# A list scheduler that orders by the array form of matmul groups and by a port that VectorE and GpSimd share

## The chip, the core and the metric

The kernel runs on one core of a Trainium2 chip. A core has a matrix engine (TensorE, PE in the views), a vector engine (VectorE, DVE), an activation engine (ScalarE, ACT), a general engine (GpSimd, POOL) and a queue engine for transfers (SyncE, SP). Each engine takes its instructions in the order in which they were written for it and waits by semaphores for what other engines make. The metric is the device time of one execution in microseconds, the median of several runs.

## The reference

What is computed, cut to what matters:

```python
# q, k, v, alpha: (4, 8, 768, 48), float32
for t in range(S):                                   # gated linear attention, per batch and head
    state = alpha[:, :, t, :, None] * state + einsum('bhd,bhe->bhde', k[:, :, t], v[:, :, t])
    y[:, :, t] = einsum('bhd,bhde->bhe', q[:, :, t], state)
x = y.transpose(0, 2, 1, 3).reshape(B, S, 384)
logits = x @ w_gate                                  # mixture: best 2 of 4 experts, softmax over the two
for e in range(4):                                   # each expert is one causal attention head of width 64
    q, k, v = x @ wq[e], x @ wk[e], x @ wv[e]
    a = softmax(causal(q @ k.T / 8))
    out += gate_weight[e] * (a @ v @ wo[e])
```

## The kernel before

**The linear attention** runs in 24 chunks of 128 time steps (4 batches of 6), all 8 heads at once, four head pairs on the partitions. For chunk `n`, `prep_r` (line 386) and `prep_c` (407) scan the gates backwards and forwards on VectorE (lines 393 and 416) and scale keys and queries with the results (420, 424). `gla_a` (439) makes the products of queries and keys on TensorE (445) into two PSUM buffers; one is masked by VectorE (454, tile `ms`), the other is copied by ScalarE (457) and masked by GpSimd (461). `gla_t` (468) transposes the keys (472), `gla_u` (480) makes the chunk's state (490; VectorE 504 or 508, GpSimd 511), and `gla_y` (515) the chunk's output (535), which is split into a high part `xh` (ScalarE, 544) and a low part `xl` (VectorE, 548) for the projections.

**The mixture** runs in 8 units of 384 rows (two for each batch; an odd unit also sees the keys of the even unit before it). `proj` (557) makes queries and keys of a pair of experts (567, nine matmuls of 384 columns), `vproj` (579) values and gate logits (585), `gate` (593) the gate weights on VectorE. For each pair of experts and each block of 128 rows `score` (625) makes the scores (642), VectorE adds the mask and takes the row's extreme (652), ScalarE takes the exponential and its sum (661), `norm` (665) makes a factor on VectorE (673, 674) and GpSimd scales the rows by it (680). `transp` (687) transposes them on TensorE (698), ScalarE copies them to `at` (712), `av` (720) multiplies them with the values (735), and `outp` (750) projects the sum (760); the result goes out by a transfer (767) from one of two buffers `ot`.

**Three forms of the matmul array.** By their `tile_position` the groups use the array in parts: 445 and 642 (in the code `pa`, `sc`) split its rows in two; 490 (`pu`) and 735 (`yv`) split its columns in two, 535 (`py`) in four; 472, 698, 567, 585 and 760 (`pt`, `tr`, `pj`, `pv`, `po`) use it whole. A float32 matmul that is no transposition counts twice in the views of the profile.

**What sets the order.** `build` (301) writes all steps down as operations of a `Plan` (59), each with its engine, an estimated occupancy and latency, and the buffers that it reads and writes. `mix` (842) interleaves the streams of operations (the rest of one unit, the projections of the next, the chunks of the one after it) by weights (`MIX_...`, lines 37 to 45); in `back` (782) the constant `AHEAD` (35) says after how many further blocks of scores a block is transposed. `schedule` (105) then plays a clock for each engine: among the operations whose inputs are there it takes, on each engine, those that could start within `LOOK` of the earliest, and of these the one that was written first. Buffers come from pools: seven PSUM buffers `g`, and SBUF pools such as `al`, `qk`, `a`, `ot`, which are given out strictly in the written order. The order in which operations are chosen is the order in which each engine gets its instructions (`emit`, 206); before the planned time 45 it fills TensorE's planned gaps with small matmuls that only keep it busy (`warm`, 941). The line that chooses:

```python
lo = min(x[0] for x in c)
t, i = min((x for x in c if x[0] <= lo + LOOK), key=lambda x: x[1])
```

## Time and profile before

| | us |
|---|---|
| median of 3 runs | 363.74 (363.12 to 364.96) |
| the profiled execution | 362.71 |
| its span, first to last instruction | 361.0 |

| engine | busy, us | share of the span | instructions |
|---|---|---|---|
| TensorE | 337.9 | 94% | 3686 |
| VectorE | 244.3 | 68% | 692 |
| ScalarE | 216.3 | 60% | 543 |
| GpSimd | 124.7 | 35% | 190 |

The profiled execution lies 1.71 us over its span and 1.03 us under the median. A share is an average over the whole span; the views by stretch, of waits and of the chain of work that ended last tell which engine the others wait for at a place. Ends of matmuls are modelled, so how long a group of matmuls holds the engine is read from the start of its first to the start of the next group's first.

### The profile page before, as it was taken

How to read it: one execution, taken by the hardware profiler on the slowest of the kernel's cores; microseconds unless marked ns; L12 is line 12 of the kernel's file. 1: busy time of each engine (PE TensorE's matmuls, PEld its weight loads, DVE VectorE, ACT ScalarE, POOL GpSimd, SP SyncE). 2: the span in 40 equal slices, each digit the busy share in tenths (PEclk: the TensorE clock that was granted, in tenths of full speed). 3: DMA queues.
4: the chain of work that ended last, by engine and by line, in shares of the span. 5: the costliest groups of instructions: out<-in, count | busy, mean ns of one | idle time of the engine just before them, and what ended most of it. 6: DMA issues, size and time to landing. Idle time of an engine off the chain costs nothing.

```text
span 361.0 us, 9454 instructions
## 1 busy us (share of the span) xinstructions
PE 337.9 (94%) x3686; PEld 264.9 (73%) x3686; DVE 244.3 (68%) x692; ACT 216.3 (60%) x543; POOL 124.7 (35%) x190
## 2 busy tenths in 40 slices
PE   8898898999899799999979999999999999999992
PEld 6678776887666587887857787877877797876682
DVE  6889999999999954665788843556266621448620
ACT  1554478754687445775548656675368564757960
POOL 4243249312485401441337321441056300423520
PEclk9999999999999989999999999999999999999997
DMA  7998333435223020423132320312100000100101
GB/s 193 272 268 213 108 108 107 134 107 149 81 78 107 27 82 27 147 78 100 35 96 83 107 58 25 118 42 70 67 3 2 2 2 3 65 1 2 65 24 54
DMA packets 13797, 29.85 MB, mean 83 GB/s; under 512 B 1616, under 2 KB 4912, under 8 KB 13744
## 3 DMA queue, kind: packets, MB, share of 16 engines
q1 hardware_dynamic: 13744, 29.16, 28.3%
q8 instruction: 31, 0.51, 0.6%
q14 instruction: 22, 0.18, 0.2%
HBM read 24.44 MB, written 4.72 MB: 81 GB/s over the span
## 4 chain that ended last, share of the span: by engine, by line
PE 54%; DVE 30%; issue 5%; ACT 4%; DMA 3%; POOL 1%; ACTq 0%; DVEq 0%; POOLq 0%
PE g L735 9%; PE g L698 9%; PE g L567 8%; PE g L642 8%; DVE al L416 6%; PE g L535 6%; PE g L760 5%; DVE al L393 5%; PE g L585 4%; DVE a L652 4%; PE g L445 3%; DVE qk L424 2%; DMA al<-in_al_dram 2%; DVE qk L420 2%; DVE ms L454 2%
## 5 line engine op out<-in xcount | busy, mean ns | idle before, releaser
L680 POOL TENSOR_SCALAR a<-a,cf,gw 128x128 f32<-128x128 f32 (+5 forms) x96 | 78.4, 827 | 130.3 <-DVE cf L674 85.8
L661 ACT ACTIVATE a<-a,mx 128x128 f32<-128x128 f32 (+5 forms) x96 | 63.2, 660 | 18.2 <-DVE mx L652 16.2
L652 DVE CUSTOM_DVE_ANT_0 a<-g,cm 128x384 f32<-128x384 f32 (+3 forms) x96 | 47.8, 530 | 35.0 <-PE g L642 30.7
L712 ACT ACTIVATE at<-g 128x512 f32<-128x512 f32 (+3 forms) x124 | 49.5, 456 | 7.8 <-PE g L698 7.7
L642 PE MATMUL g<-k,q 64*128 64x256 f32 (+3 forms) x256 | 49.7, 478 | 2.1 <-ACT ot L765 2.0
L698 PE MATMUL g<-ident,a 128*128 128x128 f32 x336 | 49.2, 283 | 1.8 <-POOL a L680 1.5
L698 PEld LDWEIGHTS g<-ident,a 128*128 128x128 f32 x336 | 38.1, 143 | 13.5 <-POOL a L680 5.1
L735 PE MATMUL g<-at,vg 128*64 128x384 f32 (+2 forms) x324 | 41.4, 393 | 1.4 <-ACT at L712 1.4
L535 PE MATMUL g<-ms,vt 128*32 128x128 f32 x768 | 36.0, 277 | 6.4 <-DVE ms L454 4.7
L436 ACT ACTIVATE al<-al 112x1033 f32<-112x1033 f32 x24 | 25.7, 1071 | 25.3 <-DVE qk L424 18.4
L393 DVE TENSOR_TENSOR_SCAN al<-al,d1r 112x516 f32<-112x516 f32 (+1 forms) x25 | 30.4, 1217 | 10.3 <-DMA al<-in_al_dram 10.3
L735 PEld LDWEIGHTS g<-at,vg 128*64 128x64 f32 x324 | 22.0, 136 | 20.3 <-issue 13.3
L567 PE MATMUL g<-xh,wqk_h 128*128 128x384 f32 x96 | 35.2, 367 | 0.5 <-DVE xl L548 0.5
L535 PEld LDWEIGHTS g<-ms,vt 128*32 128x32 f32 x768 | 23.4, 109 | 15.8 <-DVE ms L454 5.9
L567 PE MATMUL g<-xl,wqk_h 128*128 128x384 f32 x96 | 32.4, 338 | 0.5 <-DVE xl L548 0.5
L642 PEld LDWEIGHTS g<-k,q 64*128 64x128 f32 x256 | 22.5, 185 | 13.8 <-issue 4.6
L416 DVE TENSOR_TENSOR_SCAN al<-al,d1c 112x516 f32<-112x516 f32 (+1 forms) x25 | 32.1, 1283 | 0.8
L567 PE MATMUL g<-xh,wqk_l 128*128 128x384 f32 x96 | 32.4, 337 | 0.0
L511 POOL TENSOR_TENSOR S<-st,ev 48x192 f32<-48x192 f32 x32 | 21.2, 663 | 28.0 <-DVE st L508 26.8
L445 PE MATMUL g<-qk 48*128 48x128 f32 x384 | 28.1, 284 | 0.6 <-DVE qk L424 0.4
L535 PE MATMUL g<-qk,S 112*32 112x128 f32 x480 | 26.9, 275 | 0.0
L445 PEld LDWEIGHTS g<-qk 48*128 48x128 f32 x384 | 23.8, 187 | 4.0 <-issue 1.3
(91 smaller groups left out, 613.2 us busy)
## 6 DMA issues: line engine op xcount, KB each, us to landing
qk<-in_qk_dram SPq DMA_DIRECT2D x23, 448.0 KB, 4.0
vt<-in_v_dram SPq DMA_DIRECT2D x24, 256.0 KB, 4.1
al<-in_al_dram SPq DMA_DIRECT2D x23, 226.2 KB, 2.8
out_dram<-ot SPq DMA_DIRECT2D x24, 192.0 KB, 1.9
at<-in_wqk_dram SPq DMA_DIRECT2D x1, 768.0 KB, 11.4
qk<-in_qk_dram SPq DMA_DIRECT2D x2, 224.0 KB, 3.4
at<-in_wvg_dram SPq DMA_DIRECT2D x1, 390.0 KB, 10.7
at<-in_wo_dram SPq DMA_DIRECT2D x1, 384.0 KB, 11.5
```

Of the source, the lines that this page charges most:

```text
L393: V.tensor_tensor_scan(backwards(al[0:P, AW + c0 - 1:AW + c1 - 1]), backwards(al[0:P, c0:c1]), d1r[0:P, sl].rearrange("p a w -> p (a w)"), ...
L416: V.tensor_tensor_scan(c, c, T(("d1c", n))[0:P, sl].rearrange("p a w -> p (a w)"), 0.0, OP.mult, OP.max)
L445: PE.matmul(T(("pa", n, s))[:, C * p:C * p + C], t[r:r + D, p, C:2 * C], t[r:r + D, p, 0:C], start=True, stop=True, tile_position=(r, 0))
L535: PE.matmul(py[32 * j:32 * j + 32, k], l, r, start=(i == 0), stop=(i == len(parts) - 1), tile_position=(0, 32 * j))
L567: PE.matmul(pj[:, :W3], w[:, kt, cs], x[:, kt, :], start=(i == 0), stop=(i == 8))
L642: PE.matmul(T(sk[e])[:, :w], q[r, ts], k[r, c0:c1], start=True, stop=True, tile_position=(64 * e, 0))
L652: V.tensor_tensor_reduce(T(ak[e])[:, c0:c1], T(sk[e])[:, :w], cm[:, m0:m0 + w], -1.0, mx[:, 0:1] if x else BIG, OP.add, OP.min, accum_out= ...
L661: A.activation(a[:, 0:n], a[:, 0:n], AF.Exp, bias=T(mk)[:, e, len(pieces) - 1:len(pieces)], scale=-1.0, accum_out=T(("sm", u))[:, ix:ix + 1])
L680: G.tensor_scalar(a[:, 0:n], a[:, 0:n], T(ck_)[:, e:e + 1], T(("gw", u))[:, i, eg:eg + 1], op0=OP.mult, op1=OP.mult)
L698: PE.transpose(pt[:, 128 * (j - j0):128 * (j - j0) + 128], a[:, 128 * j:128 * j + 128], ident)
L712: A.activation(dst, src, AF.Copy)
L735: PE.matmul(py[64 * e:64 * e + 64, lo:n1], v[:, j % 3, 64 * eg:64 * eg + 64], at[e][:, at_off(j) + lo:at_off(j) + n1], start=(j == 0), sto ...
```

## The change

The scheduler's model is changed, and with it the order of the instructions; the operations, their sizes and their number stay the same, except for the small matmuls that fill planned gaps (88 before, 117 after).

- A TensorE operation carries the name of its form (`pe=`). `MODE` puts the forms in three classes, rows, columns and whole; between two classes the scheduler adds a time (`LEAVE` plus `ENTER`) to the start, and among the operations that could start within `LOOK` it takes one of the current class before one of another (`STICK`). The fixed 0.1 that each group's occupancy held before is gone.
- A VectorE operation with `port=True` and every GpSimd operation take turns on one modelled port (`port_at`).
- `use=` names the buffers of an operation's product, the one that a later operation copies out of PSUM: they are claimed with the operation itself, and other users of the buffer follow that one (`claims`).
- Successors on the same engine other than TensorE wait for the end of the latency (`SAME`); some occupancies are changed; the start of the plan (`ISSUE`) goes from 3.0 to 0.9.
- `AHEAD` goes from 3 to 2, and the weights of `mix` are other ones.

```diff
-AHEAD = 3
+AHEAD = 2
-MIX_BACK = (12, 20, 12, 20, 14, 20)
-MIX_FRONT = (16, 9, 11, 10, 12, 9)
+MIX_BACK = (10, 20, 8, 19, 13, 20)
+MIX_FRONT = (17, 7, 13, 10, 12, 9)
...
-MIX_GLA = 12
+MIX_GLA = 25
...
-ISSUE = 3.0
+ISSUE = 0.9
 SEM = 0.07
+SAME = 0.02
+STICK = 100
...
+MODE = {"pa": "row", "sc": "row", "pu": "col", "py": "col", "yv": "col"}
+ENTER = {"pa": 0.10, "sc": 0.104, "py": 0.024, "pu": 0.0, "yv": 0.05, "tr": 0.055, "pt": 0.055}
+LEAVE = {"pu": 0.064, "py": 0.11}
...
-    def op(self, eng, occ, lat, fn, r=(), w=(), dma=0):
+    def op(self, eng, occ, lat, fn, r=(), w=(), use=(), dma=0, port=False, pe=None):
...
+        keys += [k for k in use if k not in keys]
...
-            self.touch.setdefault(k, []).append(i)
+            t = self.touch.setdefault(k, [])
+            if t and k[0] in self.kinds:
+                claims.add(t[0])
+            t.append(i)
...
+        state = ["pj"]
+
+        def change(o):
+            a, b = state[0], o["pe"]
+            if MODE.get(a) == MODE.get(b):
+                return 0.0
+            return LEAVE.get(a, 0.096) + ENTER.get(b, 0.105)
...
             t = max(rt[i], at[o["eng"]])
+            if o["port"]:
+                t = max(t, port_at)
+            if o["pe"]:
+                t = max(rt[i], t + change(o))
...
-                    t, i = min((x for x in c if x[0] <= lo + LOOK), key=lambda x: x[1])
+                    c = [x for x in c if x[0] <= lo + LOOK]
+                    if e == "PE":
+                        t, i = min(c, key=lambda x: x[1] + STICK * (MODE.get(ops[x[1]]["pe"]) != MODE.get(state[0])))
+                    else:
+                        t, i = min(c, key=lambda x: x[1])
...
+            if o["port"]:
+                port_at = max(port_at, end - 0.03)
+            if o["pe"]:
+                state[0] = o["pe"]
...
-                op("PE", m * 0.109 + 0.1, m * 0.109 + 0.27, f, r=[(("a", u, pair, i, e), "s"), (("ident",), None)],
-                   w=whole(tk) + [(("at", u, pair, e), "slot")])
+                op("PE", m * 0.109, m * 0.109 + 0.17, f, pe="tr", r=[(("a", u, pair, i, e), "s"), (("ident",), None)],
+                   w=whole(tk), use=[("at", u, pair, e)])
```

**Two places in the order.** The first is TensorE at the last scores of unit 1 (`k_105` and `q_103` are the second pair's keys and queries, `a_136` the scaled rows that are transposed, 445 and 480, 535 and 571, 642 and 679 the same lines before and after). Before:

```order
L698 MATMUL g_67<-ident,a_136 128x128 x4
L698 MATMUL g_66<-ident,a_136 128x128
L642 MATMUL g_63<-k_105,q_103 128x256
L642 MATMUL g_64<-k_105,q_103 128x256
L642 MATMUL g_65<-k_105,q_103 128x512
L642 MATMUL g_69<-k_105,q_103 128x512
L535 MATMUL g_68<-ms_90,vt_80 32x128 x4
L535 MATMUL g_68<-qk_76,S_94 32x128 x4
L535 MATMUL g_68<-ms_90,vt_80 32x128 x4
L535 MATMUL g_68<-qk_76,S_94 32x128 x4
L535 MATMUL g_68<-ms_90,vt_80 32x128 x8
L535 MATMUL g_68<-qk_76,S_94 32x128 x4
```

and in the changed kernel:

```order
L480 MATMUL g_68<-qk_77 128x128
L480 MATMUL g_69<-qk_77 128x128
L679 MATMUL g_65<-k_105,q_103 128x512
L679 MATMUL g_67<-k_105,q_103 128x512
L679 MATMUL g_63<-k_105,q_103 128x256
L679 MATMUL g_64<-k_105,q_103 128x256
L679 MATMUL g_66<-k_106,q_100 128x128
L679 MATMUL g_69<-k_106,q_100 128x128
L571 MATMUL g_68<-ms_90,vt_80 32x128 x4
L571 MATMUL g_68<-qk_76,S_94 32x128 x4
L571 MATMUL g_68<-ms_90,vt_80 32x128 x4
L571 MATMUL g_68<-qk_76,S_94 32x128 x4
```

These scores now follow products of a chunk (480) and are followed by the next unit's first scores, all of the form with split rows; before they stood between transpositions and a chunk's output, one score block in its form by itself.

The second is VectorE ahead of the masked products of chunk 11 (`ms_91` in both). Before, with the forward scan of chunk 17 (`al_71`) ahead of it:

```order
L393 SCALAR_TENSOR_TENSOR al_71<-al_71,d1r 112x516
L397 RECIPROCAL d1c_87<-al_71 112x4
L416 SCALAR_TENSOR_TENSOR al_71<-al_71,d1c_87 112x516
L745 TENSOR_TENSOR yl_143<-g_67,yh_141 128x384
L454 TENSOR_TENSOR ms_91<-g_66,mask 128x512
```

and in the changed kernel, where `al_71` holds chunk 13 and `al_72` chunk 14 (428 and 451 are the scans, 544 the state, 781 the low part of a unit's output, 489 the masked products):

```order
L451 SCALAR_TENSOR_TENSOR al_71<-al_71,d1c_87 112x516
L428 SCALAR_TENSOR_TENSOR al_72<-al_72,d1r 112x516
L544 TENSOR_TENSOR st_93<-g_66,S_94 48x192
L781 TENSOR_TENSOR yl_143<-g_67,yh_141 128x384
L489 TENSOR_TENSOR ms_90<-g_64,mask 128x512
L544 TENSOR_TENSOR st_93<-g_66,S_94 48x192
L489 TENSOR_TENSOR ms_91<-g_68,mask 128x512
```

VectorE's preparation of chunks runs six chunks ahead of the masked products before, and three after.

## Rows read from the trace of the kernel before

**Rows 1.** The page's first part: busy time, share of the span and instructions of each engine.

```profile
PE 337.9 (94%) x3686; PEld 264.9 (73%) x3686; DVE 244.3 (68%) x692; ACT 216.3 (60%) x543; POOL 124.7 (35%) x190
```

**Rows 2.** Busy time of each engine in four stretches of the span: to the first projection, to the output of chunk 11, to the last matmul of the output, and the end. Columns: length, then busy time and number of instructions of PE, PEld, DVE, ACT and POOL, the granted clock as a share of full speed, DMA share and GB/s.

```profile
0.00:26.80 26.80, 23.18 (x341) 18.33 (x341) 21.07 (x36) 11.07 (x19) 9.26 (x27) 1.00 0.93 244
26.80:127.20 100.40, 91.03 (x1079) 71.79 (x1076) 97.72 (x231) 61.25 (x150) 44.68 (x58) 1.00 0.40 110
127.20:354.10 226.90, 223.49 (x2268) 174.72 (x2268) 125.39 (x426) 143.46 (x374) 70.72 (x106) 0.99 0.17 53
354.10:361.00 6.90, 0.21 (x3) 0.09 (x2) 0.15 (x1) 0.49 (x1) 0.00 (x0) 0.71 0.14 43
```

**Rows 3.** The chain of work that ended last, in order of time, where it passes from VectorE to TensorE: start, length, what.

```profile
124.42 1.55 DVE al L416
126.56 0.61 DVE ms L454
127.21 2.26 PE g L535 x56
129.48 4.09 PE g L698 x26
```

**Rows 4.** Timeline of TensorE about 325 us: start, modelled length, operation, sizes, count. A pair of scores of 512 columns is x4, one of 256 columns x4 too.

```profile
323.12 1.13 PE L642 MATMUL g<-k,q 64*128 64x512 f32 x4
324.18 0.55 PE L698 MATMUL g<-ident,a 128*128 128x128 f32 x3
...
327.38 2.42 PE L642 MATMUL g<-k,q 64*128 64x512 f32 x12
329.73 0.65 PE L698 MATMUL g<-ident,a 128*128 128x128 f32 x4
```

**Rows 5.** The chain of work again, from 196 to 219 us, where every piece is TensorE's: start, length, line and number of matmuls.

```profile
196.88 0.70 PE g L642 x4
197.58 1.28 PE g L585 x9
...
201.84 1.46 PE g L698 x12
203.30 1.09 PE g L585 x9
...
205.98 3.38 PE g L735 x24
209.36 1.77 PE g L567 x9
...
211.56 1.68 PE g L535 x56
213.24 1.13 PE g L698 x9
214.37 1.57 PE g L567 x9
215.95 1.86 PE g L698 x17
```

**Rows 6.** Timeline of TensorE at two places where the same group of 735 is followed by two others, of two and of four column parts.

```profile
159.77 1.52 PE L735 MATMUL g<-at,vg 128*64 128x384 f32 x12
161.11 0.53 PE L490 MATMUL g<-vt,kt 128*48 128x48 f32 x16
...
72.50 1.52 PE L735 MATMUL g<-at,vg 128*64 128x384 f32 x12
73.95 0.43 PE L535 MATMUL g<-ms,vt 128*32 128x128 f32 x8
```

**Rows 7.** Timeline of TensorE, two rows with the idle time before them and what ended it.

```profile
127.21 0.43 PE L535 MATMUL g<-ms,vt 128*32 128x128 f32 x8 [3.08 <-DVE ms L454]
...
184.03 1.55 PE L642 MATMUL g<-k,q 64*128 64x512 f32 x6 [1.97 <-ACT ot L765]
```

**Rows 8.** Stretches of 2 us behind the first of these waits, columns as in Rows 2.

```profile
128.00:130.00 2.00, 2.00 (x39) 1.61 (x32) 1.71 (x3) 0.47 (x1) 0.00 (x0) 0.57 0.03 8
...
132.00:134.00 2.00, 2.00 (x19) 2.00 (x18) 0.00 (x0) 2.00 (x7) 0.00 (x0) 1.00 0.57 180
```

**Rows 9.** VectorE's work for a chunk, groups by line and shape: operation, names, shapes, count, busy us, mean ns of one, idle us before and what ended it.

```profile
L416 DVE TENSOR_TENSOR_SCAN al<-al,d1c 112x516 f32<-112x516 f32 x23 | 30.5, 1328 | 0.8
L393 DVE TENSOR_TENSOR_SCAN al<-al,d1r 112x516 f32<-112x516 f32 x23 | 29.0, 1263 | 9.3 <-DMA al<-in_al_dram 9.3
L420 DVE TENSOR_TENSOR qk<-qk,al 112x512 f32<-112x512 f32 x23 | 17.2, 749 | 6.1 <-DMA qk<-in_qk_dram 6.0
L424 DVE TENSOR_TENSOR qk<-qk,al 112x512 f32<-112x512 f32 x23 | 16.3, 709 | 0.0
```

**Rows 10.** Groups by line and shape on the way from the scores to the transpositions, for rows of 768 columns, columns as in Rows 9.

```profile
L680 POOL TENSOR_SCALAR a<-a,cf,gw 128x768 f32<-128x768 f32 x16 | 16.5, 1043 | 19.7 <-DVE cf L674 9.9 <-ACT at L712 4.7 <-PE g L642 2.7
L661 ACT ACTIVATE a<-a,mx 128x768 f32<-128x768 f32 x16 | 14.8, 927 | 2.4 <-DVE mx L652 2.0
L652 DVE CUSTOM_DVE_ANT_0 a<-g,cm,mx 128x256 f32<-128x256 f32 x32 | 14.3, 476 | 0.0
L661 ACT ACTIVATION_READ_ACCUMULATOR a<-a,mx 128x1 f32 x96 | 18.0, 188 | 0.0
L673 DVE TENSOR_SCALAR cf<-sm 128x2 f32<-128x2 f32 x48 | 9.8, 204 | 13.9 <-ACT a L661 13.7
```

More of the change, by code (lines that the diff above doesn't have):

```diff
@@ L98, in op @@
         for k in keys:
-            self.touch.setdefault(k, []).append(i)
-        self.ops.append(dict(i=i, eng=eng, occ=occ, lat=lat, fn=fn, preds=preds, keys=keys, dma=dma))
+            t = self.touch.setdefault(k, [])
+            if t and k[0] in self.kinds:
+                claims.add(t[0])
+            t.append(i)
+        self.ops.append(dict(i=i, eng=eng, occ=occ, lat=lat, fn=fn, preds=preds, claims=claims - preds, keys=keys, dma=dma, pe=pe,
+                             port=port or eng == "G"))
         if eng == "PE":
@@ L123, in schedule @@
         for o in ops:
-            miss.append(len(o["preds"]))
-            for j in o["preds"]:
+            miss.append(len(o["preds"]) + len(o["claims"]))
+            for j in o["preds"] | o["claims"]:
                 succ[j].append(o["i"])
@@ L192, in schedule @@
             for j in succ[i]:
-                same = ops[j]["eng"] == e and not o["dma"]
-                rt[j] = max(rt[j], t + o["occ"] if same else end + SEM)
+                if i in ops[j]["claims"]:
+                    rt[j] = max(rt[j], t)
+                elif ops[j]["eng"] != e or o["dma"]:
+                    rt[j] = max(rt[j], end + SEM)
+                else:
+                    rt[j] = max(rt[j], t + o["occ"] if e == "PE" else end + SAME)
                 miss[j] -= 1
@@ L294, in pol @@
     def pol(n):
-        return 0.3 + n / 1150, 0.32 + n / 1150
+        return 0.31 + n / 1150, 0.33 + n / 1150
     def whole(*keys):
@@ L398, in prep_r @@
             occ = 0.08 + (c1 - c0) * 0.00206
-            op("V", occ, occ + 0.09, f, r=[(("al", n), ("c", p)) for p in ps_] + whole(("d1r",)),
+            op("V", occ, occ + 0.09, f, port=True, r=[(("al", n), ("c", p)) for p in ps_] + whole(("d1r",)),
                w=[(("al", n), ("s", p)) for p in ps_])
@@ L446, in f @@
                                   start=True, stop=True, tile_position=(r, 0))
-            op("PE", 1.1, 1.3, f, r=[(("qk", n), (x, p)) for x in "kq" for p in range(4)],
-               w=whole(("pa", n, 0), ("pa", n, 1)))
+            op("PE", 0.9, 1.17, f, pe="pa", r=[(("qk", n), (x, p)) for x in "kq" for p in range(4)],
+               w=whole(("pa", n, 0), ("pa", n, 1)), use=[("ms", n)])
             for s in (0, 1):
@@ L475, in g @@
                 A.activation(T(("kt", n)), T(("pt", n))[:, 0:4 * P].rearrange("p (a b) -> p a b", a=4), AF.Copy)
-            op("PE", 0.485, 0.65, f, r=[(("qk", n), ("k", p)) for p in range(4)] + whole(("ident",)),
-               w=whole(("pt", n)))
+            op("PE", 0.385, 0.55, f, pe="pt", r=[(("qk", n), ("k", p)) for p in range(4)] + whole(("ident",)),
+               w=whole(("pt", n)), use=[("kt", n)])
             op("A", *act(448), g, r=whole(("pt", n)), w=whole(("kt", n)))
@@ L540, in gla_y @@
                 r += whole(("S", n))
-            op("PE", occ, occ + 0.17, f, r=r, w=whole(("py", n)))
+            op("PE", occ, occ + 0.17, f, r=r, pe="py",
+               w=whole(("py", n)), use=[("xh", u), ("xl", u)])
             def fh(T):
@@ L568, in f @@
                         i += 1
-            op("PE", 1.67, 1.83, f, r=xs(u) + [(("wqk_h",), None), (("wqk_l",), which)],
-               w=whole(("pj", u, pair, which)))
+            op("PE", 1.57, 1.73, f, pe="pj", r=xs(u) + [(("wqk_h",), None), (("wqk_l",), which)],
+               w=whole(("pj", u, pair, which)), use=[("k", b, pair) if which else ("q", u, pair)])
             if which == 0:
@@ L643, in f @@
                                   tile_position=(64 * e, 0))
-                occ = 2 * (0.008 + w / 1200) + 0.1
-                wr = whole(*sk)
-                if x == 0:
-                    wr = wr + [(ak[0], "slot"), (ak[1], "slot"), (mk, "slot")]
-                op("PE", occ, occ + 0.17, f, r=whole(("q", u, pair)) + [(("k", b, pair), h) for h in range(hf + 1)], w=wr)
+                occ = 2 * (0.008 + w / 1200)
+                op("PE", occ, occ + 0.17, f, pe="sc", r=whole(("q", u, pair)) + [(("k", b, pair), h) for h in range(hf + 1)],
+                   w=whole(*sk), use=ak + [mk])
                 for e in (0, 1):
@@ L674, in f @@
                 V.reciprocal(cf, cf)
-            op("V", 0.24, 0.3, f, r=[(("sm", u), i0), (("sm", u), i0 + 3)], w=whole(ck_))
+            op("V", 0.29, 0.36, f, r=[(("sm", u), i0), (("sm", u), i0 + 3)], w=whole(ck_))
             for e in (0, 1):
@@ L737, in f @@
                                   start=(j == 0), stop=(j == nj - 1), tile_position=(0, 64 * e))
-            occ = 0.1 + sum(2 * (0.008 + (n1 - max(n0, 128 * (j - 3 * hf))) / 1200) for j in range(nj))
+            occ = sum(2 * (0.008 + (n1 - max(n0, 128 * (j - 3 * hf))) / 1200) for j in range(nj))
             r = whole(*[("vg", 2 * b + h) for h in range(hf + 1)])
@@ L741, in av @@
                   if j0 < 3 * hf + i + 1]
-            op("PE", occ, occ + 0.17, f, r=r, w=whole(yk))
+            op("PE", occ, occ + 0.17, f, r=r, pe="yv",
+               w=whole(yk), use=[("yh", u, pair), ("yl", u, pair)])
             op("A", *act(n1 - n0), lambda T: A.activation(T(("yh", u, pair))[:, ns], T(yk)[:, ns], AF.Copy),
@@ L762, in f @@
                         m += 1
-            op("PE", 1.14, 1.3, f, r=[((x, u, pair), i) for x in ("yh", "yl") for pair in (0, 1)]
-               + whole(("wo_h",), ("wo_l",)), w=whole(("po", u, i)))
+            op("PE", 1.05, 1.22, f, pe="po", r=[((x, u, pair), i) for x in ("yh", "yl") for pair in (0, 1)]
+               + whole(("wo_h",), ("wo_l",)), w=whole(("po", u, i)), use=[("ot", u, i)])
             op("A", *act(W3), lambda T: A.activation(T(("ot", u, i)), T(("po", u, i))[:, 0:DM], AF.Copy),
```

51 lines of the change are left out of this document (26 added, 25 removed).

## Prediction

> **What bounds the kernel now.** I read the page's busy shares first [rows 1]: TensorE is busy 94% of the span, VectorE 68%, so TensorE is the first suspect; but a share is a mean, so the stretches come next [rows 2]. To 127.2 us VectorE is the busier one: of the 100.4 us behind the first projection it works 97.7 and TensorE 91.0. Behind that TensorE works 223.5 of 226.9 us and VectorE 125.4. The chain of waits says the same: it runs through VectorE's scans until the masked products of chunk 11, and through TensorE from 127.21 on [rows 3]. There TensorE had stood idle for 3.08 us [rows 7], and in the 2 us from 128 its granted clock was 0.57, between the levels 1.2 and 2.4 GHz, and 1.00 again from 132 [rows 8]. So there are two stretches with different limits, VectorE's to 127.2 and TensorE's to 354.1, and 6.9 us of ending that no step here touches.
>
> A busy TensorE isn't one that computes all the time. A pair of scores of 512 columns alone takes 324.18 - 323.12 = 1.06 us from start to next start; a run of two such pairs and one of 256 columns takes 329.73 - 327.38 = 2.35 [rows 4]. With g for the pair and s for what a run costs however long it is, g + s = 1.06 and 2.5 g + s = 2.35: g = 0.86, s = 0.20. That s is the price of changing the array's form.
>
> **The change part by part.** No computation is removed, so everything hangs on the order.
>
> *Changes of form.* I counted in the two orders how often a TensorE group follows one of another form, with two and four column parts as two forms: 201 before, 96 after. The prices are from the chain, whose pieces run from the end of one group to the end of the next, so that the whole price lies in the group entered [rows 5]. Values' projections take 1.28 us behind scores and 1.09 behind transpositions; queries' and keys' projections 1.77 behind 735 and 1.57 behind transpositions: 0.19 to 0.20. Nine transpositions behind 535 take 1.13, and seventeen behind a projection 1.86, which is 0.109 each, so nine should take 0.98: 0.15. Scores, and likewise the products of a chunk, cost 0.20 [rows 4]. The column forms are priced by 735, which takes 73.95 - 72.50 = 1.45 us when the four-part 535 follows, and 161.11 - 159.77 = 1.34 when the two-part 490 follows [rows 6]: 0.11, and I take 0.12. By what is entered: rows split, 62 to 23, 39 x 0.20 = 7.8; projections, 32 to 11, 21 x 0.195 = 4.1; transpositions, 47 to 14, 33 x 0.15 = 5.0; columns split, 60 to 48, 12 x 0.12 = 1.4. Together 18.3 us of TensorE. With every change at the cheapest price (0.11) it would be 11.6, with every one at 0.20 21.0. Up to the output of chunk 11 the count falls from 71 to 35 (6.3 us at these prices), behind it from 130 to 61 (12.0 us).
>
> The scheduler's own classes hold two and four column parts for one form, and by them the counts are 193 and 78. Those rows show that a change between them costs the same 0.11. The Trainium skill's page "TensorEngine Tiling (Array Packing)", section Tiling Modes, says that changing the tiling mode, not just the tile, drains TensorE, and lists 128x64 and 128x32 as different configurations; the rows agree, and by the scheduler's classes the saving would be 115 changes, some 1.2 us more.
>
> *What stands ahead of chunk 11 on VectorE.* It was the later engine there. In the new order there stand ahead of `ms` of chunk 11 three reverse and four forward scans fewer (3 x 1.263 + 4 x 1.328 = 9.1 us), two pairs of products with keys and queries fewer (2 x 1.458 = 2.9) [rows 9], and four reductions of scores (0.476 for the shape in rows 10), four reciprocals, an `xl` and a pair of factors, some 3: 15 us in all. Up to 127.2 VectorE stood idle 26.8 - 21.1 + 100.4 - 97.7 = 8.4 us [rows 2]; with the same idle time it reaches that point at 127.2 - 15 = 112.2.
>
> *What stands ahead of chunk 11 on TensorE.* The same groups but for one projection, one score block and five transposition groups more, which comes to 3.3 us moved forward (1.57 for the projection [rows 5], some 1.7 for the rest at 0.109 a transposition and 0.86 for 512 columns of scores), and 36 changes of form fewer. TensorE idled 100.4 - 91.0 = 9.4 us there. Without any of it, it reaches chunk 11's output at 127.2 - 6.3 + 3.3 - 9.4 = 114.8; with all of it at 124.2. VectorE's 112.2 is no longer the later one, but two engines that are loaded alike, and wait for each other's buffers, lose some: I take a third of the 9.4 back, **118**. The ends are 114.8 and 124.2. The first 26.8 us hang on VectorE, busy for 21.1 of them [rows 2], whose order hardly moves there, and stay; the 29 more filling matmuls are written only where the plan has a gap, and I put them at nothing; where there is no gap they cost 0.107 us each, a quarter of the 0.43 that the four passes of a 256-column pair take [rows 4], 3.1 us at most.
>
> *Behind chunk 11.* 226.9 - 12.0 - 3.3 = 211.6. Of the idle 3.4 us there, 1.97 stood behind a transfer out of `ot` [rows 7]; the new claims let an output projection start only when its `ot` is free, so other groups go ahead. The clock's fall cost the 26 transpositions 4.09 - 26 x 0.109 = 1.25 us [rows 3], which goes with the wait that caused it. Against these 3.2 stands the shorter look-ahead (`AHEAD` 2): from a block's last scores to its transpositions TensorE's other work is, by order and durations, an estimate of 7.9 us in the middle and 4.1 at the least, before 11.7 and 3.1. For 768 columns the way between takes at least 0.48 (reduction) + 2 x (0.93 + 0.19 to read the sum out) + 0.40 (factor and its reciprocal, taken as equally long) + 1.04 (scaling) = 4.2 us [rows 10], and more when an engine is held up. I put some 4 us of new waits there. So 211.6 - 3.2 + 4.4 = 212.8, with the tight groups' waits between 0 and 12.
>
> **Sum.** 118 + 212.8 = 330.8 for the last matmul in place of 354.1: 23.3 us less. The profiled execution took 362.71 and would take 339.4; the median, 1.03 above it, **340.4**.
>
> **The rivals.**
>
> *VectorE stays the bound in the first stretch.* For it: it had only 2.7 idle us in 100, and scans are stretched when GpSimd works beside them (1.55 us in rows 3 against a mean of 1.33), which an order doesn't forbid. Then chunk 11 is reached at some 125, and waits of 4 us more follow behind it since units come late: 125 + 216.8 = 341.8 for the last matmul, 12.3 less: 351. Against it: 15 us of its work move behind that point by the order itself.
>
> *Still more is gained.* If the two engines mesh in the first stretch (114.8) and no wait comes behind it (211.6 - 3.2 = 208.4): 323.2, 30.9 less, 333. The rows speak against so smooth a run: TensorE had 9.4 us of waits there even with VectorE working throughout.
>
> *Slower: the softmax doesn't come back in time.* With look-ahead 2, and scores gathered in runs, a run's blocks reach VectorE, ScalarE and GpSimd together, and the last of them comes back latest; the transpositions at the head of TensorE's queue hold up everything behind them, the projections too. The 24 blocks of the odd units have the longest way (4.2 us and more, as above, against an estimate of 4 to 9 of cover). The gain of 23.3 is gone when each waits 0.97 us longer; at 1.5 us each it is 340.4 + 36 = 376, and idle times as long as the one at 127 would bring the clock's fall as well. Against it: where the way is longest the cover is mostly longer, and a wait once taken gives the next blocks time.
>
> *No change.* It would need the waits to grow by just what the changes of form give. That the kernel doesn't do what it says is excluded for the order, which shows 96 changes.
>
> **How the numbers follow.** The forecast's neighbourhood (335 to 346) 0.5; below 335 0.13; VectorE's bound or more waits (346 to 362) 0.25; no change 0.04; slower 0.08. A measurement of this kernel tells about 0.5% from no change, 1.8 us; faster by more than that has 0.88, within it 0.04, slower 0.08. The range leaves out the best end of the gain and what is slower than a bit beyond the first rival: 331 to 355.
>
> **What would show it.** Right: in the chain, projections at 1.57 and 1.09 far more often than at 1.77 and 1.28; runs of scores; the output of chunk 11 at about 118; no VectorE row ahead of it with a wait of 3 us; TensorE's busy time near 338 - 18.3 + 3.1 = 323 or less. Wrong: TensorE's groups of 698 waiting for GpSimd's 680 for more than 5 us in all (the slower rival), VectorE still busy for 97 in 100 us and TensorE waiting for 454 or 548 (the first rival), or changes of form that cost less in runs than alone.

## The result and the profile after

The changed kernel takes 329.98 us (median of 4 runs, 328.62 to 331.35), the kernel before on the same chip 363.43 (4 runs): a ratio of 0.9076, 95% interval 0.9026 to 0.9126, 33.4 us less. The profiled execution took 328.62 us, its span is 326.9. The forecast was 340.4 with a range of 331 to 355: the direction is right, and the gain is 10 us larger than forecast, 1 us outside the range.

The page's first part, which answers to [rows 1]:

```profile
PE 317.0 (97%) x3715; PEld 265.0 (81%) x3715; DVE 239.7 (73%) x692; ACT 214.3 (66%) x543; POOL 134.3 (41%) x190
```

TensorE works 20.9 us less, VectorE 4.6 and ScalarE 2.0 us less, and GpSimd 9.6 us longer. The same four stretches as in [rows 2] (to the first projection, here one of values, to the output of chunk 11, to the last matmul of the output, the end), with the same columns:

```profile
0.00:26.93 26.93, 25.38 (x369) 20.66 (x370) 22.41 (x38) 12.09 (x20) 9.41 (x28) 1.00 0.93 249
26.93:111.80 84.87, 84.44 (x1106) 73.81 (x1107) 80.86 (x208) 57.84 (x147) 40.59 (x53) 1.00 0.41 115
111.80:319.46 207.66, 207.04 (x2251) 170.53 (x2243) 136.26 (x446) 143.86 (x377) 84.27 (x110) 1.00 0.21 62
319.46:326.90 7.44, 0.12 (x2) 0.01 (x2) 0.14 (x1) 0.49 (x1) 0.00 (x0) 0.66 0.20 66
```

The reader is to see three things. The second stretch is 15.5 us shorter and TensorE is idle for 0.4 us of it, not 9.4. The third is 19.2 us shorter, idle 0.6, not 3.4. And the clock is at its upper level until the last matmul; the fall of [rows 8] is gone with the wait ahead of it. The whole list of the waits that show as TensorE's idle time (waiting line, releaser, us in all, times, longest):

```profile
PE pw L979 <- POOL d1r L388: 1.6, 1, 1.6
PE g L507 <- DVE st L544: 0.4, 1, 0.4
PE g L733 <- DVE mx L687: 0.2, 1, 0.2
```

The wait for the masked products and the one behind `ot` [rows 7] don't stand in it any more. The outputs of chunks 10 and 11 now run one behind the other, in one form (timeline of TensorE; the row at 111.80 begins chunk 11's):

```profile
110.24 0.43 PE L571 MATMUL g<-ms,vt 128*32 128x128 f32 x8
...
111.80 0.41 PE L571 MATMUL g<-ms,vt 128*32 128x128 f32 x8
...
113.46 1.16 PE L480 MATMUL g<-qk 48*128 48x128 f32 x16
```

The chain of work, which answers to [rows 4, 5]: start, length, line, number of matmuls.

```profile
28.27 3.13 PE g L604 x18
31.78 2.18 PE g L622 x18
...
150.34 0.70 PE g L679 x4
151.04 1.76 PE g L604 x9
...
285.81 2.78 PE g L679 x16
```

Two projections in a row take 2 x 1.57 and two of values 2 x 1.09, the cheap lengths of [rows 5]; one behind scores still pays (1.76). By the order the groups of scores now come in 28 runs, 7 of them a group alone; before it was 41 runs and 25 alone. The last row is a run of four groups, 16 matmuls.

**Where the time went.** Idle rows don't tell all that TensorE loses. A matmul's end is modelled: here, in the kernel before, the last projection matmul ends 0.34 us after its start by the profile, although in a run the next one starts 0.17 to 0.18 after it, so the idle time behind it (1.19) is counted from too late a point:

```profile
41.40 0.34 PE L567 MATMUL g<-xl,wqk_h 128*128 128x384 f32 x1
41.57 0.34 PE L567 MATMUL g<-xh,wqk_l 128*128 128x384 f32 x1
43.10 0.43 PE L535 MATMUL g<-ms,vt 128*32 128x128 f32 x8 [1.19 <-DVE ms L454]
```

So I went by starts. From the time between the first start of each TensorE group and that of the next, over eight of the kernels below together, a time for each kind of matmul was fitted, and a price for leaving and for entering a form; what a group takes beyond that is waiting. (Groups next to filling matmuls are left out, so 190 and 83 changes are counted of 201 and 96.) The matmuls themselves come to 271.1 us before and 271.0 after. The changes of form cost 31.0 us before and 13.7 after, 0.16 each. The waits come to **22.6 us before, of which the idle rows show 12.8 (9.4 and 3.4, [rows 2]), and 4.3 after**. Of the 34.6 us by which the last matmul comes earlier (354.1 to 319.5), forms are 17.3, waits 18.3, and the rest (fillers, the beginning) goes 1.0 the other way. The level of the waits depends on the fit, the difference hardly: when it is made to count more or fewer groups as waiting, the waits come to between 21.8 and 25.4 us before and between 3.3 and 7.9 after, and the difference to between 17.5 and 18.5.

### The profile page after: what moved, and what is told of

Read it like the earlier page. It is cut to its first block, busy times and chain, and to the rows that moved or that the text cites. A ratio compares the mean times of both kernels' runs of the same rounds, so it can differ in the third digit from the quotient of the medians.

```text
span 326.9 us, 9547 instructions
## 1 busy us (share of the span) xinstructions
PE 317.0 (97%) x3715; PEld 265.0 (81%) x3715; DVE 239.7 (73%) x692; ACT 214.3 (66%) x543; POOL 134.3 (41%) x190
## 4 chain that ended last, share of the span: by engine, by line
PE 92%; DVE 4%; POOL 1%; ACT 1%; issue 0%; POOLq 0%; ACTq 0%; DVEq 0%
PE g L604 15%; PE g L679 11%; PE g L571 11%; PE g L733 11%; PE g L770 10%; PE g L796 8%; PE g L622 8%; PE g L480 7%; PE pw L979 5%; PE g L525 3%; PE g L507 2%; DVE a L687 1%; POOL a L715 1%; DVE al L451 0%; DVE qk L455 0%
## 5 line engine op out<-in xcount | busy, mean ns | idle before, releaser
L715 POOL TENSOR_SCALAR a<-a,cf,gw 128x128 f32<-128x128 f32 (+5 forms) x96 | 88.7, 936 | 62.9 <-DVE cf L709 43.1
L733 PE MATMUL g<-ident,a 128*128 128x128 f32 x336 | 46.3, 275 | 0.5 <-DVE mx L687 0.2
L679 PE MATMUL g<-k,q 64*128 64x256 f32 (+3 forms) x256 | 43.8, 454 | 0.0
L770 PE MATMUL g<-at,vg 128*64 128x384 f32 (+2 forms) x324 | 39.5, 391 | 0.0
L770 PEld LDWEIGHTS g<-at,vg 128*64 128x64 f32 x324 | 20.9, 137 | 18.3 <-issue 14.4
L571 PE MATMUL g<-ms,vt 128*32 128x128 f32 x768 | 33.2, 275 | 0.1
L679 PEld LDWEIGHTS g<-k,q 64*128 64x128 f32 x256 | 23.9, 186 | 9.4 <-issue 4.7
L451 DVE TENSOR_TENSOR_SCAN al<-al,d1c 112x516 f32<-112x516 f32 (+1 forms) x25 | 30.6, 1223 | 0.5
L496 POOL TENSOR_SCALAR_AFFINE_SELECT ms<-ms 128x512 f32<-128x512 f32 x24 | 16.2, 675 | 33.2 <-ACT ms L492 32.6
L480 PE MATMUL g<-qk 48*128 48x128 f32 x384 | 26.2, 278 | 0.0
L571 PEld LDWEIGHTS g<-ms,vt 128*32 128x32 f32 x768 | 20.6, 109 | 5.3 <-issue 2.3
## 6 DMA issues: line engine op xcount, KB each, us to landing
at<-in_wqk_dram SPq DMA_DIRECT2D x1, 768.0 KB, 11.1
```

The source lines that it names most:

```text
L451: V.tensor_tensor_scan(c, c, T(("d1c", n))[0:P, sl].rearrange("p a w -> p (a w)"), 0.0, OP.mult, OP.max)
L480: PE.matmul(T(("pa", n, s))[:, C * p:C * p + C], t[r:r + D, p, C:2 * C], t[r:r + D, p, 0:C], start=True, stop=True, tile_position=(r, 0))
L571: PE.matmul(py[32 * j:32 * j + 32, k], l, r, start=(i == 0), stop=(i == len(parts) - 1), tile_position=(0, 32 * j))
L679: PE.matmul(T(sk[e])[:, :w], q[r, ts], k[r, c0:c1], start=True, stop=True, tile_position=(64 * e, 0))
L715: G.tensor_scalar(a[:, 0:n], a[:, 0:n], T(ck_)[:, e:e + 1], T(("gw", u))[:, i, eg:eg + 1], op0=OP.mult, op1=OP.mult)
L733: PE.transpose(pt[:, 128 * (j - j0):128 * (j - j0) + 128], a[:, 128 * j:128 * j + 128], ident)
```

## The experiments

The theory A behind the forecast: the gain is TensorE's changes of form, and the waits go with the new order. The rivals: the new weights of `mix` made it (B), or the other parts of the scheduler's model did, the modelled port and the early claims (C). Each run has its time, and the split of TensorE's time as above:

| run | what differs | us | changes, us | waits, us |
|---|---|---|---|---|
| kernel before | | 363.4 | 31.0 | 22.6 |
| e1 | before, new weights | 358.92 | 31.0 | 18.9 |
| e7 | before, scans held back | 360.17 | 31.5 | 19.2 |
| h1 | before, early claims | 361.81 | 30.5 | 21.9 |
| h2 | before, new weights and the plan's new times | 347.33 | 30.5 | 5.9 |
| g2 | h2 and early claims | 345.76 | 32.6 | 2.5 |
| e3 | g2 and port (all but forms) | 347.09 | 32.6 | 1.6 |
| e4 | g2 and forms (all but port) | 341.17 | 13.4 | 17.2 |
| e5 | e4, scans held back | 353.40 | 13.3 | 29.5 |
| e6 | e4, longer GpSimd durations | 335.88 | 13.6 | 11.1 |
| e9 | all but early claims | 342.99 | 15.7 | 15.3 |
| changed kernel | | 329.98 | 13.7 | 4.3 |
| e2 | changed, old weights | 331.26 | 14.0 | 4.6 |
| g1 | changed, AHEAD 3 | 331.70 | 14.6 | 4.8 |
| g3 | changed, four-column class | 329.63 | 13.3 | 4.0 |
| g4 | changed, one price 0.12 | 333.80 | 16.0 | 4.7 |

The kernel before took 363.1 to 363.6 us beside them on each chip. A run's 95% interval reaches some 1 to 2 us either way, so rows nearer to each other than some 2 us are not told apart.

### The weights: e1 and e2

```diff
# e1, on the kernel before (e2 is the reverse, on the changed kernel)
-AHEAD = 3
+AHEAD = 2
-MIX_BACK = (12, 20, 12, 20, 14, 20)
+MIX_BACK = (10, 20, 8, 19, 13, 20)
...
-MIX_GLA = 12
+MIX_GLA = 25
```

> The kernel before with nothing but the changed kernel's constants (look-ahead 2 and the new weights of mix). Its order has 199 changes of form (before 201, changed kernel 96). Theory A, the scheduler's knowledge of the forms brings the gain, and the waits go because TensorE's groups no longer stand one by one: 358 to 366 us. Rival B, the constants bring the part of the gain that is not the price of the forms (about 15 us of waits): 345 to 351.

> The changed kernel with all constants of before (look-ahead 3, old weights). 97 changes of form. Theory A: 328 to 335 us. Rival B: about 345, since the waits of before would come back with the constants.

e1: 358.92 us, ratio 0.9893 (0.9854 to 0.9932). e2: 331.26, ratio 0.9131 (0.9092 to 0.9170). The weights are worth 4.2 us on the old scheduler and 1.3 on the new one, where the intervals overlap; B falls.

### The forms: e3

```diff
-MODE = {"pa": "row", "sc": "row", "pu": "col", "py": "col", "yv": "col"}
+MODE = {}
```

> The changed kernel with an empty table of forms: no price and no preference for the form in force; port, claims and constants as changed. 207 changes of form by the order. If a change of form costs what the rows gave (0.11 to 0.20 us) and nothing else depends on it, 330 + 19.6 = 350 us (theory C: the waits went by the port and the claims). If the waits come back with the forms (theory A), 360 to 366. If changes of form were free and all came from waits, 330.

347.09 us, ratio 0.9551 (0.9517 to 0.9584), with 207 changes, 111 more than in the changed kernel: 17.1 us slower. That is a net figure: by the split the changes take 18.9 us more and the waits 2.7 less. A expected the waits to come back as well. They did not; the waits view of e3 without the start:

```profile
PE g L622 <- DVE wv_l L381: 0.4, 1, 0.4
PE g L733 <- ACT at L747: 0.4, 1, 0.4
```

So the half of the gain that is no change of form comes without any knowledge of forms. That half of A fell here.

### The port: e4, e5 and e6

```diff
# e4
-                             port=port or eng == "G"))
+                             port=False))
```

> The changed kernel with no operation marked for the shared port. 94 changes of form; VectorE's preparation runs up to six chunks ahead of the masked products again, as in the kernel before. Theory A: 328 to 333 us. Theory C, the port's modelling keeps VectorE from being the bound: 337 to 346, with TensorE waiting for VectorE's masked products.

341.17 us, ratio 0.9394 (0.9361 to 0.9426): 11.2 us slower than the changed kernel at two changes of form fewer, so C had the time right here. It had the wait wrong: it named VectorE's masked products (489), and TensorE's transpositions wait mostly for GpSimd's scaling (the first rows of the waits view without the start):

```profile
PE g L733 <- POOL a L715: 4.5, 6, 1.6
...
PE g L679 <- DVE ms L489: 1.0, 1, 1.0
PE g L733 <- DVE xl L585: 0.6, 1, 0.6
```

Two readings were open. Without the port VectorE scans up to six chunks ahead (R), or the plan doesn't know that GpSimd's scalings last longer beside the scans (D). Scalings of 128 columns, planned at 0.42 us (0.31 + 128/1150), in e4 and in the changed kernel (busy, mean ns, idle before):

```profile
L715 POOL TENSOR_SCALAR a<-a,cf,gw 128x128 f32<-128x128 f32 x16 | 11.6, 732 | 0.1
```

```profile
L715 POOL TENSOR_SCALAR a<-a,cf,gw 128x128 f32<-128x128 f32 x16 | 9.8, 622 | 2.2 <-DVE cf L709 1.4 <-ACT a L696 0.8
```

These means mix two cases. In the changed kernel 13 of the 16 take 0.44 to 0.46 us, some of them beside other work of VectorE, and the three that run beside a chunk's scan or its products with keys and queries (455, 459) take 1.24 to 1.46; in e4 11 take 0.44 to 0.46 and five 0.77 to 1.87. Two scalings in a row in the changed kernel, and what VectorE does beside the second:

```profile
211.10 0.46 POOL L715 TENSOR_SCALAR a<-a,cf,gw 128x128 f32<-128x128 f32 x1
211.53 1.41 POOL L715 TENSOR_SCALAR a<-a,cf,gw 128x128 f32<-128x128 f32 x1
```

```profile
211.42 0.68 DVE L455 TENSOR_TENSOR qk<-qk,al 112x512 f32<-112x512 f32 x1
212.02 0.68 DVE L459 TENSOR_TENSOR qk<-qk,al 112x512 f32<-112x512 f32 x1
```

```diff
# e5, on e4, ahead of the scheduling (scan: the reverse scan's operation; masked: VectorE's at the masked products)
+    for n, i in pl.scan.items():
+        if n - 3 in pl.masked:
+            pl.ops[i]["preds"].add(pl.masked[n - 3])
# e6, on e4
-        return 0.31 + n / 1150, 0.33 + n / 1150
+        return 0.52 + n / 1150, 0.54 + n / 1150
...
-                    op("G", 0.64, 0.7, f2, w=[(("ms", n), s)])
+                    op("G", 0.71, 0.77, f2, w=[(("ms", n), s)])
```

> The changed kernel without its modelled port (as in the run without the port, 341.2 us), and the reverse scan of chunk n may go on VectorE only behind the masked products of chunk n-3. The order then has VectorE's preparation at most 2 chunks ahead of the masked products (6 without the port, up to 4 by chunk 16 in the changed kernel) and the same 94 changes of form. Theory R (the modelled port pays because it keeps VectorE from scanning far ahead, so that masked products and softmax steps come in time): 330 to 334 us. Theory D (it pays because the plan then knows that GpSimd's scalings take longer beside VectorE's scans, so that transpositions are put behind them at a greater distance; how far ahead the scans run is nothing): 338 to 343 us, with TensorE still waiting some 4 us for GpSimd's scaling (715).

> The changed kernel without its modelled port, and GpSimd's operations are planned at the durations that the trace of the run without the port shows (a scaling 0.21 us longer, the mask 0.71 for 0.64, the state 0.69 for 0.52, the copy of the gates 0.48 for 0.17). 98 changes of form; VectorE's preparation runs up to 7 chunks ahead. Theory D (the plan must know how long GpSimd takes): 330 to 335 us, the waits for 715 gone. Theory R (the run-ahead costs): 338 to 343 us.

e5: 353.40 us, ratio 0.974 (0.970 to 0.978), 12.2 us slower than e4 and outside what either reading gave. R fails for a hold this tight (two chunks; the changed kernel runs up to four ahead, and a looser hold was not tried). But the other half of D, that how far ahead the scans run is nothing, fails too: held back, scans and chunk products meet more scalings (counted from the traces, 32 of the 96 overlap one by over 0.2 us and take 27.0 us longer than without it; in e4 26 and 20.3), and the transpositions' waits for the scaling (lines 734 and 716 in this kernel) triple. The mean granted clock is 0.975, 0.992 in e4:

```profile
PE g L734 <- POOL a L716: 13.9, 15, 1.8
```

e6: 335.88 us, ratio 0.9251 (0.9216 to 0.9287), 5.3 of the 11.2 us back, and that wait shrinks:

```profile
PE g L733 <- POOL a L715: 0.8, 3, 0.4
```

D is right for about half. It expected up to 335 us; a longer mean fits neither of the two lengths above, while the port says when the two meet (that this makes the other half is argued, not shown). The port is no cure for the meetings themselves: in the changed kernel 26 scalings meet a scan or a chunk product and lose 20.8 us in all, as in e4, but in its list of waits no transposition waits for one.

### The scans on the old scheduler: e7

The same three lines as in e5, on the kernel before.

> The kernel before, with one thing added: the reverse scan of chunk n may go on VectorE only behind the masked products of chunk n-3. Changes of form stay (204 for 201). The prediction's step for the first stretch (VectorE works up to six chunks ahead, and TensorE waits behind it): most of the 9.4 us idle up to chunk 11 goes, 353 to 358 us. The rival (the scans are only moved, and others come to be waited for): 360 to 365 us.

360.17 us, ratio 0.9901 (0.9866 to 0.9936): 3.4 us, in the rival's range. But the first stretch does gain. Its row, with the columns of [rows 2], ends at the output of chunk 11, and TensorE has done the same matmuls (x1079) 6.2 us earlier:

```profile
26.72:121.01 94.29, 89.11 (x1079) 72.15 (x1076) 85.69 (x217) 60.21 (x147) 43.79 (x55) 1.00 0.40 112
```

By starts TensorE's waits ahead of that output fall from 14.0 to 7.5 us, and behind it they rise by some 3. So VectorE's work ahead held about half of the first stretch's waits; holding it back moves a part of them behind chunk 11, and to GpSimd's half of the masked products (the whole run):

```profile
PE g L536 <- POOL ms L462: 4.3, 5, 2.0
PE g L536 <- DVE ms L455: 1.7, 2, 1.2
```

### The claims: e8, e9, g2, h1 and h2

```diff
# e9, and h2 with the diffs of e3 and e4 (e8: this and the next)
-        keys += [k for k in use if k not in keys]
# e8
-                claims.add(t[0])
```

> The changed kernel without the claims: the buffers of a TensorE operation's product are claimed only with the operation that copies it out. 103 changes of form for 96, which at 0.15 us each is 1 us. If the claims carry a part of the waits that went: 334 to 340 us, with TensorE waiting for ScalarE's or VectorE's copies. If they carry nothing: 329.5 to 332 us.

In e8 the users of a buffer no longer follow the one that claims it, so one of them can overwrite content that is still wanted: it computes something else, and its time, 343.93 us, ratio 0.9464 (0.9428 to 0.9500), carries no conclusion. e9 keeps the followers and only claims with the copy:

> The changed kernel, where the buffer of a TensorE operation's product is claimed with the operation that copies it out, as in the kernel before, and other users still follow that one. 107 changes of form for 96, which at 0.15 us each is 1.7 us. If the early claims carry a part of the waits that went: 335 to 341 us, with TensorE waiting for buffers or copies. If they carry nothing: 330 to 333 us.

342.99 us, ratio 0.9439 (0.9402 to 0.9476): 13.0 us slower, by the split 2.0 of it changes and 11.0 waits. The mechanism, where the largest waits of e9 stand (some 6 us from 207 to 217; the others were not followed), in ScalarE's timeline and TensorE's: the product of a projection (604), made by 201.4, waits in PSUM for its copy (609) until scores (679) have read the former `q`; ScalarE, which takes its instructions in order, stands for 2.55 us behind that copy, and the next scores wait for the copied `q`.

```profile
208.25 0.49 ACT L609 ACTIVATE q<-g 128x384 f32<-128x384 f32 x1 [2.55 <-PE g L679]
```

```profile
208.79 0.49 PE L679 MATMUL g<-k,q 64*128 64x128 f32 x4 [0.58 <-ACT q L609]
...
211.61 1.22 PE L679 MATMUL g<-k,q 64*128 64x256 f32 x2 [0.57 <-DVE ms L489]
```

In the changed kernel no copy of `q` waits for scores, only for its own projection. e9 goes further back than the kernel before, in which scores and transpositions already claimed their own buffers (`a`, `mx`, `at`). What the claims do without forms and port, and without the plan's new durations, took three more runs:

> The changed kernel without forms (MODE empty) and without the modelled port: of the three parts of the model only the early claims are left. 207 changes of form. If the claims take waits away by themselves: 345 to 352 us. If port and claims are only worth something together: 354 to 360 us, as the kernel before with the new weights (358.9).

> The kernel before with the early claims alone (use= at the TensorE operations, and other users of a buffer follow the one that claims it); old durations, old weights, no forms, no port. 198 changes of form for 201. If the claims take the waits away: 345 to 352 us. If the plan's durations do: 358 to 364 us.

> The changed kernel without forms, port and early claims: what is left is the new weights, the new durations of VectorE's and GpSimd's operations and the rule for successors on the same engine. 196 changes of form. If the durations take the waits away: 345 to 350 us, as with the claims (345.8). If the claims do: 355 to 360 us, as the old scheduler with the new weights (358.9).

g2 (the diffs of e3 and e4 together) takes 345.76 us, ratio 0.952 (0.9484 to 0.9556). That looked like the claims. h1 speaks against it: with the claims alone the old scheduler takes 361.81 us, ratio 0.9953 (0.9928 to 0.9978), 1.3 us less. And h2, with no claims, forms or port, takes 347.33, ratio 0.9552 (0.9528 to 0.9576). From e1 to h2 the plan's times change (the occupancies, the 0.1 that every TensorE group held, `SAME`, `ISSUE`), and the claims only backwards, as in e9: 11.6 us, 13.0 of waits. Its waits view without the start, first three rows, against those of h1:

```profile
PE g L571 <- POOL ms L496: 0.9, 1, 0.9
PE g L507 <- DVE qk L455: 0.5, 1, 0.5
PE g L733 <- POOL a L715: 0.2, 1, 0.2
```

```profile
PE g L543 <- POOL ms L468: 4.3, 4, 3.3
PE g L543 <- DVE ms L461: 1.9, 3, 1.2
```

One of these durations in the changed kernel's trace; the plan has 0.36 for it, and had 0.275:

```profile
L544 DVE TENSOR_TENSOR st<-g,S 48x192 f32<-48x192 f32 x32 | 11.3, 353 | 5.2 <-PE g L525 3.9 <-POOL S L547 0.4 <-ACT at L747 0.4
```

But the new times are not truer throughout. Added up from each `kernel.py`, VectorE's planned occupancies rise from 217.4 us (e1) to 227.8 (h2), and TensorE's fall from 324.3 to 283.1, where the fit gives some 314 in both (282 for the matmuls, 32 for the changes, groups next to fillers included). So the old plan has TensorE 10 us too slow and h2's, without the 0.1 and without prices for forms, 31 us too fast. Whether the waits go because products are planned more truly, or because TensorE arrives later than planned, was not tried. What h2 does show is that this half of the gain needs neither port nor claims, so C falls there.

### What a change of form costs: f1, f2 and f3

```diff
# f2; in the middle of each of the 80 groups of 604, 622 and 796
+                PE.matmul(pw[:, 0:128], zb[0:64, 0:128], zb[0:64, 0:128], start=True, stop=True, tile_position=(0, 0))
# f1: zb[:, 0:128] for both, no tile_position; f3: pw[0:64, 0:128] <- zb[:, 0:64], zb[:, 0:128]
```

> The changed kernel with one extra matmul of 128 columns (bfloat16, into the filler's buffer) in the middle of each of the 80 groups of projections, values and outputs (604, 622, 796), in their own form, on the whole array. The filler of 256 columns takes 0.12 us from start to start in the changed kernel, so one of 128 some 0.06: 5 us for 80, 335 us. It is the base for the next two.

> The same 80 extra matmuls of 128 columns, but with 64 rows of the array (tile_position (0, 0)), so that TensorE goes into the form with split rows and out of it 80 times in the middle of a group: 160 changes. The prediction's prices (0.20 into rows, 0.195 back to projections): 0.395 us for a pair, 31.6 us over the run with whole matmuls. By the run without classes (17.1 us for 111 changes, 0.154 each): 24.6 us. If what that run lost is order and not form: under 6 us.

> The same 80 extra matmuls, with 64 columns of the array for their output. The prediction's prices (0.12 into columns, 0.195 back): 0.315 us for a pair, 25.2 us over the run with whole matmuls; by the mean of the run without classes 24.6 us. If form costs nothing here: under 6 us.

f1: 340.17 us, ratio 0.9347 (0.9311 to 0.9384); f2: 358.76, 0.9869 (0.9828 to 0.9911); f3: 359.87, 0.9900 (0.9863 to 0.9937). Over f1 that is 18.6 and 19.7 us for 80 pairs, 0.232 and 0.246 a pair, 0.116 and 0.123 a change. All three expectations were off: the base costs 10.2 us and not 5, and the pairs less than either estimate; that form costs nothing (under 6 us) is refuted. A projection about the extra matmul (596), in f1, f2 and f3:

```profile
61.30 0.33 PE L608 MATMUL g<-xh,wqk_h 128*128 128x384 f32 x1
61.47 0.23 PE L596 MATMUL pw<-d1r 128*128 128x128 bf16 x1
61.51 0.42 PE L608 MATMUL g<-xl,wqk_h 128*128 128x384 f32 x1
61.77 0.34 PE L608 MATMUL g<-xh,wqk_l 128*128 128x384 f32 x1
```

```profile
60.40 0.33 PE L608 MATMUL g<-xh,wqk_h 128*128 128x384 f32 x1
60.67 0.23 PE L596 MATMUL pw<-d1r 64*128 64x128 bf16 x1
60.82 0.45 PE L608 MATMUL g<-xl,wqk_h 128*128 128x384 f32 x1
61.10 0.34 PE L608 MATMUL g<-xh,wqk_l 128*128 128x384 f32 x1
```

```profile
60.15 0.33 PE L608 MATMUL g<-xh,wqk_h 128*128 128x384 f32 x1
60.41 0.24 PE L596 MATMUL pw<-d1r 128*64 128x128 bf16 x1
60.59 0.44 PE L608 MATMUL g<-xl,wqk_h 128*128 128x384 f32 x1
60.87 0.34 PE L608 MATMUL g<-xh,wqk_l 128*128 128x384 f32 x1
```

From the first row to the last it is 0.47, 0.70 and 0.72 us. In f2 the extra matmul starts 0.27 after the projection's and not 0.17, and the next one 0.15 after it and not 0.04: both ways are paid, about evenly. Part of what a change brings is in the base, too: a whole extra matmul costs 0.127 where its columns take an estimated 0.05 to 0.06, half of a filler's. With that 0.07 a pair is 0.30 to 0.32, near the 0.16 a change of the fit. That this is the reason is argued, not shown; the extra matmul also differs in type and buffer from the group about it.

### The look-ahead, a finer class, one price: g1, g3 and g4

```diff
# g1
-AHEAD = 2
+AHEAD = 3
# g3
-MODE = {"pa": "row", "sc": "row", "pu": "col", "py": "col", "yv": "col"}
+MODE = {"pa": "row", "sc": "row", "pu": "col", "py": "col4", "yv": "col"}
# g4
-            return LEAVE.get(a, 0.096) + ENTER.get(b, 0.105)
+            return 0.12
```

> The changed kernel with AHEAD back at 3: a block's transpositions come after three further blocks of scores in the written order, not two. 101 changes of form for 96, some 0.6 to 0.8 us. The prediction's term (the shorter look-ahead costs 4.4 us of waits behind chunk 11): 326 to 329 us. What the trace after shows (no wait of transpositions, so nothing to give back): 330 to 333 us.

> The changed kernel with the output of a chunk (571, four column parts) as a class of its own; the trace of before showed a price of 0.11 us between two and four column parts. 93 changes of form for 96. If the true forms pay: 327 to 329.5 us. If three changes are lost in the rest of the order: 329.5 to 332 us.

> The changed kernel with one price for every change of form in the plan, 0.12 us, as the runs with extra matmuls give it (0.116 and 0.123), in place of LEAVE plus ENTER (0.05 to 0.21). 107 changes for 96, at 0.12 to 0.17 us some 1.3 to 1.9 us more: 331 to 333 us. If a plan with truer prices waits less: 326 to 329 us.

g1: 331.70 us, ratio 0.9139 (0.9104 to 0.9175): not faster (1.7 us slower, where the intervals overlap), and by starts its waits are no fewer, 4.8 us for 4.3; the shorter look-ahead costs no wait that the longer one saves. g3: 329.63, ratio 0.9081 (0.9047 to 0.9115): no difference from the changed kernel that can be measured. g4: 333.80, ratio 0.9186 (0.9146 to 0.9227), with 11 changes more: 3.8 us slower, somewhat beyond what either expectation gave. No run beat the changed kernel measurably.

## Why the prediction was wrong

**The changes of form: right.** 18.3 us forecast, 17.3 by the fit; against e3 18.9 for the changes, 17.1 net, since the changed kernel waits 2.7 us more than e3. The price of 0.20 for a single score block [rows 4] and those of [rows 5] carried the term; the extra matmuls give less for one change (0.12) in the middle of a projection, 12.6 us for 105, and the difference is not settled.

**The waits: the step that failed.** The forecast took 9.4 us of idle time away in the first stretch and put 3.2 back, and behind chunk 11 took 3.2 away and put 4.4 on for the look-ahead: -5.0 us in all. Measured: -18.3. It failed in two ways. *The size*: idle rows were taken for all that TensorE loses. By starts it loses 14.0 us before chunk 11 and 8.7 behind it, not 9.4 and 3.4. That is why 111.80 lies even ahead of the best end (114.8), and 207.66 ahead of 208.4. *What stands against it*: the 3.2 and the 4.4 were put back by judgement, and the trace after has 0.5 us of waits in the first stretch and 3.8 behind it. So of the 13.3 us, 10.0 are waits that the forecast didn't see in the kernel before (it took 12.6 away, and 22.6 were there), and 3.3 are waits that it put back and that didn't come (7.6 for 4.3). The 4.4 was near in size: by starts the largest waits left behind chunk 11 stand at transpositions that follow scores, about 2.5 us in all at 186 and 290. But its cause was wrong, since g1 (`AHEAD` 3) has no fewer.

**Where the waits went** was not asked, since the forecast gave the plan's new times no term at all; their line in the change reads like housekeeping. By e1 and h2 they take 13.0 us of waits away while the scheduler knows nothing of forms, with the new weights in both; that they are truer is not shown. Then each part changes its worth with the others. Forms without the port gain 4.6 us (g2 to e4: 19.2 less for changes, 14.7 more waits), with it 17.1 (e3 to the changed kernel). The port without forms is worth nothing (g2 to e3, 1.3 slower), with them 11.2; the claims 1.3 to 1.6 without forms (h1; h2 to g2, where the intervals overlap), with forms and port up to 13.0 (e9, which claims even later than the kernel before). A reason that fits: gathering by form shortens TensorE's work between a block's scores and its transpositions (by the order and the durations an estimate of 11.4 us in the middle in g2, 7.1 in e4, 7.8 in the changed kernel), so that a late scaling or a blocked buffer is waited for. Which of the new durations counts most was not tried.

**VectorE in the first stretch: the amount right, its role half right.** Up to the output of chunk 11 its work fell by 15.5 us (118.8 to 103.3), 15 forecast. But e7, which takes nothing but the work ahead away, brings that output 6.2 us earlier and not 15, and the whole gains 3.4: the engine with the larger share set about half of the waits there, and the rest had other releasers. Its scans last about as long as in [rows 9]:

```profile
L451 DVE TENSOR_TENSOR_SCAN al<-al,d1c 112x516 f32<-112x516 f32 x23 | 29.1, 1265 | 0.4
L428 DVE TENSOR_TENSOR_SCAN al<-al,d1r 112x516 f32<-112x516 f32 x23 | 28.8, 1258 | 1.4 <-DMA al<-in_al_dram 1.4
```

**The rivals.** VectorE as the bound (351) and the slow softmax (376) did not come; the latter would have shown in 733 waiting for 715, as in e5. "Still more is gained" (333) was the nearest, and it had the right place, the waits of both stretches, but took them from the idle rows as well. The 29 further fillers cost next to nothing: the beginning is 0.1 us longer.

## What to carry to other kernels

Measure what an engine loses to waits by the starts of its work, against the same work where it runs freely; idle time by modelled ends showed 12.8 of 22.6 us here. In a list scheduler look at the planned times early: here new ones alone were worth 11.6 us, the model of TensorE's forms 17.1 on top of port and claims, and forms paid fully only once port and claims kept the closer order from waiting (4.6 us without the port). And look at single lengths and not at a mean: 622 ns stood for 0.45 and 1.4 us. Take parts out of the old version and of the new one both: claims were worth 1.3 us in the one and up to 13.0 in the other.

## What was not expected of the hardware

A matmul of 128 bfloat16 columns in the middle of a float32 group, of the same form, costs 0.127 us, twice its columns' time. GpSimd's scaling of 128 columns takes 0.44 to 0.46 us in the changed kernel, also beside other work of VectorE, and 1.24 to 1.46 beside VectorE's scans and chunk products. The scans suffer less: 1.22 us on the mean alone and 1.30 beside GpSimd. And the kernel with more GpSimd time in all (134.3 us against 124.7) is the faster one: such meetings cost little where the plan leaves room for them.
